# Output products of an attention and maxout kernel: one full-mode matmul, or four column tiles of 32 tokens

## The chip, the cores and the metric

The kernel runs on one core of a Trainium2 chip. The metric is device time in microseconds of one execution. A profile is taken of one execution; its span runs from the first to the last instruction of the program, and the execution's own time is a little longer.

## The reference

Two attention blocks with 32 inducing points, then a layer that takes the larger of two linear maps and multiplies it by a third.

```python
def _attn_ref(x, inducing):            # x: 4 x 12544 x 128, inducing: 32 x 128
    def mab(q, kv):
        s = scale * (q @ kv.transpose(0, 2, 1))
        a = np.exp(s - s.max(-1, keepdims=True))
        a /= a.sum(-1, keepdims=True) + 1e-09
        return a @ kv
    h = mab(I, x)                      # 32 rows a batch
    return mab(x, h)                   # 12544 rows a batch
def _moe_ref(x, w1, w2, w_out):        # x: 50176 x 128, w1, w2: 128 x 1024, w_out: 1024 x 128
    g = np.maximum(x @ w1, x @ w2)
    return g @ w_out
```

## The kernel before

max(a, b) = a + relu(b - a), so the result is x @ (w1 @ w_out) + relu(x @ (w2 - w1)) @ w_out. The kernel works with `w21 = w2 - w1` and `w1out = w1 @ w_out`. As the second attention's output is a weighted sum of the 32 rows of `h`, `h @ w21` (`hwd`) and `h @ w1out` (`m1`) are made once a batch, and the exponentials `e2` of the second attention's scores are multiplied by them without being divided first; the divisor `rp` is applied when the output leaves PSUM, since relu commutes with a positive factor.

For each of the 4 batches the first pass (`pool_scores` L356, `pool_turn` L395, `pool_accum` L414, in batch 0 `p1_transpose` L276, `p1_scores` L292, `p1_accum` L319 and L328) makes `h`, and the small steps `pool_rest` L380, `small_rep` L459, `small_h` L489, `small_hwd` L521 and `small_m1` L554 make what the second pass needs. For batches 1 to 3 this is woven into the second pass of the batch before.

The second pass goes over blocks of up to 16 chunks of 128 tokens; a block has four quarters, one for each strip of 32 rows of the TensorE array. Its steps are these.

- `stage` (L657, column tiles): scores of a block, then the exponentials on ScalarE.
- `phase` (L1085, row tiles 32 x 128): up to four relu inputs `hwd` x `e2` at once, one for each quarter; the linear part `m1` x `e2` of an output group (`linear_of`) rides along in such a phase or, for the last groups, in `linear_full` (L909). Each result is evicted from PSUM with a relu, by ScalarE (L1102) or VectorE (L1105).
- `final_one` (L932): one output product, 128 tokens of relu by one block of 128 rows of `w_out`, added to its group's PSUM bank. The relu tile is the stationary operand, so the output has tokens on partitions. A group of w chunks takes 8 w such products. There are 3,136 of them: 392 chunks by 8.
- `evict_group` (L964, or L971): the group leaves PSUM multiplied by `rp` and is stored (L989).
- `dens` (L764) makes divisors on TensorE for a few blocks; for the others `turn_e2` does it by a DMA transpose (L711) and additions on GpSimd (L720, L724).

The order on TensorE is written out by hand in `ORDER`, a list of words: `p3.2` is a phase with three jobs (and a mask that moves evictions between ScalarE and VectorE), a number is that many calls of `final_one`, `s` a stage, and the other letters are the steps named above. A `Clock` keeps estimated times of all engines while the program is recorded: its constants `PAIR` (one product) and `SWITCH` (a change of the array's tile shape) add up TensorE's time, and from the estimates the planner picks the PSUM bank, the engine of each eviction, the order of the matmuls within a phase, whether a linear part is ready, and whether `keep_busy` puts filling matmuls (L891) into a wait.

Of the kernel before, what the change touches and what calls it, by code (L numbers as in the profile page):

```python
# [20 lines left out]
class Clock:  # L21


    PAIR = 0.0558
    SWITCH = {"full": 0.11, "row": 0.097, "col": 0.097}
    LAT = 0.20
    ROW = 0.224
# [19 lines left out]
    def run(self, us, mode="full", ready=0.0, why="data"):  # L47
        if mode != self.mode:
            self.pe += self.SWITCH[mode]
            self.busy["sw"] = self.busy.get("sw", 0) + self.SWITCH[mode]  # L50
            self.mode = mode
# [80 lines left out]
def kernel(  # L132
# [9 lines left out]
    nc = tc.nc  # L142
# [3 lines left out]
    NJB = J // 128  # L146
# [22 lines left out]
    ck = Clock()  # L169
    uid = [0]  # L170

    def bank(shape, dtype=F32, only=None):
        i = min(range(8), key=lambda j: ck.bank[j]) if only is None else only
        uid[0] += 1
        return i, psum.tile(shape, dtype, name=f"ps{uid[0]}", tag=f"bank{i}", bufs=1)
# [55 lines left out]
    woutp = consts.tile([128, NJB, C], F16, name="woutp")  # L231
# [6 lines left out]
    with tc.manual_schedule(engines={ET.PE, ET.DVE, ET.Activation, ET.Pool, ET.SP}):  # L238
# [402 lines left out]
        state = {}  # L641
# [107 lines left out]
        def dens(blk):  # L749

            blks = [blk]
            if 0 < blk.index < len(blocks) - 1:
                nxt = blocks[blk.index + 1]
                if nxt.staged is not None and nxt.staged <= ck.pe and nxt.rp is None:
                    blks.append(nxt)
            bi, ps = bank([128, 512])
            ck.wait(ck.bank[bi], "den bank")
            uid[0] += 1
            rp = rpp.tile([128, 8, 4], F32, name=f"rp_{uid[0]}", tag="rp")
            n = 0  # L760
            for blk in blks:
                wd = blk.width
                for t in range(wd):
                    nc.tensor.matmul(  # L764
                        out=ps[:, 4 * (n + t) : 4 * (n + t) + 4],
                        lhsT=blk.e2[:, 128 * t : 128 * (t + 1)],
                        rhs=ones_q,
                        start=True,
                        stop=True,
                    )  # L770
                blk.rp = rp[:, n : n + wd, :]
                n += wd
            end = ck.run(0.029 * n)
            nc.vector.reciprocal(out=rp[:, 0:n, :].rearrange("p t q -> p (t q)"), in_=ps[:, 0 : 4 * n])
            ck.bank[bi] = ck.on_dve(end, 0.18 + 0.001 * 4 * n)
# [103 lines left out]
        def keep_busy(until):  # L879

            g = groups[state["g"]] if state["g"] < len(groups) else None
            if held:
                g = held[0]
            elif g is None or not g.started:
                return
            turn = ck.SWITCH["full"] if ck.mode != "full" else 0.0
            n = int((until - ck.pe - turn - 0.1) / 0.11)
            if n < (3 if turn else 1):
                return
            for _ in range(n):  # L890
                nc.tensor.matmul(  # L891
                    out=g.ps[:, 0 : 128 * min(2, len(g.chunks))],
                    lhsT=warm[:, 0:128],
                    rhs=warm[:, 0 : 128 * min(2, len(g.chunks))],
                    start=False,
                    stop=False,
                    skip_group_check=True,
                )
            ck.run(0.11 * n)
# [3 lines left out]
        def linear_full():  # L903

            g = held[0]
            if st[g.blk.b].get("m1r", INF) > ck.pe or "m1" not in st[g.blk.b]:
                return False
            for s, (q, t) in enumerate(g.chunks):
                nc.tensor.matmul(  # L909
                    out=g.ps[:, 128 * s : 128 * (s + 1)],  # L910
                    lhsT=g.blk.e2[:, 128 * t : 128 * (t + 1)],
                    rhs=m1bd[:, q, :],
                    start=False,
                    stop=True,
                    skip_group_check=True,
                )
            evict_group(held.pop(0), ck.run(0.056 * len(g.chunks)))
            return True

        def final_one():  # L920
            g = groups[state["g"]]
            n = len(g.chunks)
            if g.blk.rp is None:
                dens(g.blk)
            if g.ps is None:
                g.bank, g.ps = bank([128, 512])
                ck.wait(ck.bank[g.bank], "group bank")
                ck.bank[g.bank] = INF
            jb, t = g.order[state["mm"]]
            c = g.chunks.index((g.q, t))  # L930
            w4 = g.blk.quarters[g.q].w
            nc.tensor.matmul(  # L932
                out=g.ps[:, 128 * c : 128 * (c + 1)],
                lhsT=g.blk.relu[g.q][:, 128 * (jb * w4 + t) : 128 * (jb * w4 + t + 1)],
                rhs=woutp[:, jb, :],
                start=not g.started,
                stop=(state["mm"] + 1 == n * NJB and g.linear),
                skip_group_check=True,
            )
            g.started = True  # L940
            end = ck.run(ck.PAIR)
            state["mm"] += 1
            state["done"] += 1
            if state["mm"] == n * NJB:
                if g.linear:
                    evict_group(g, end)
                else:
                    held.append(g)
                    if g.full:
                        linear_full()  # L950
                state["g"] += 1
                state["mm"] = 0

        def evict_group(g, end):
            n = len(g.chunks)
            uid[0] += 1
            osb = outp.tile([128, 4, C], F32, name=f"o_{uid[0]}", tag="o")
            q, t0 = g.chunks[0]
            who = int(EVICT[g.index])
            m = (n, 0)[who]  # L960
            end = max(end, g.blk.divided, ck.stored.pop(0))
            done = 0.0
            if m:
                nc.vector.tensor_mul(  # L964
                    osb[:, 0:m, :],
                    g.ps[:, 0 : m * C].rearrange("p (s c) -> p s c", s=m),
                    g.blk.rp[:, t0 : t0 + m, q : q + 1].broadcast_to((128, m, C)),
                )
                done = ck.on_dve(end, 0.066 + m * 128 / 960.0)
            for k in range(m, n):  # L970
                nc.scalar.activation(  # L971
                    out=osb[:, k, :],
                    in_=g.ps[:, k * C : (k + 1) * C],
                    func=AF.Copy,
                    scale=g.blk.rp[:, t0 + k, q : q + 1],
                )
                done = max(done, ck.on_act(end, 0.25))
            ck.bank[g.bank] = done
            runs = []
            for s, (q, t) in enumerate(g.chunks):  # L980
                qu = g.blk.quarters[q]
                c = qu.c0 + t
                if runs and runs[-1][0] == qu.b and runs[-1][1] + runs[-1][3] == c:
                    runs[-1][3] += 1
                else:
                    runs.append([qu.b, c, s, 1])
            for b, c, s, m in runs:
                stored = ck.on_sp(ck.bank[g.bank], 0.6)
                nc.sync.dma_start(out=outr[b, :, c : c + m, :], in_=osb[:, s : s + m, :])  # L989
            ck.stored.append(stored)  # L990
# [40 lines left out]
        def phase(n, flip=0):  # L1031
# [9 lines left out]
            if ck.mode != "row":  # L1041
                if got:
                    keep_busy(got[0][5] - ck.SWITCH["row"])
                ck.pe += ck.SWITCH["row"]
                ck.mode = "row"
# [112 lines left out]
        for word in ORDER.split():  # L1158
            if word == "s":
                stage(blocks[state["stage"]])  # L1160
                state["stage"] += 1
            elif word.isdigit():
                for _ in range(int(word)):
                    ready = final_ready()
                    keep_busy(ready)
                    ck.wait(ready, "relu")
                    final_one()
            else:
                WORK[word[0]](*[int(n) for n in word[1:].split(".") if n])
# [32 lines left out]
```

## Time and profile before

| | |
|---|---|
| median of 2 runs | 318.06 us (317.67 to 318.45) |
| profiled execution | 317.76 us |
| its span | 316.0 us |
| TensorE busy | 308.6 us, 98% |
| ScalarE, VectorE, GpSimd busy | 280.2, 274.5, 125.8 us |
| granted TensorE clock, mean | 0.998 |
| products (L932) | 3,136 matmuls, 219 ns each, 203.5 us busy |
| relu evictions | 470 on ScalarE (627 ns), 314 on VectorE (684 ns) |

Busy time counts each stretch of time once, however many matmuls overlap in it. A single matmul's duration is a modelled latency; the time that it costs in a row of matmuls is the distance from one start to the next.

### The profile page before, as it was taken

What the parts mean: (1) busy time and instruction counts of PE and PEld (TensorE: products, weight loads), DVE (VectorE), ACT (ScalarE), POOL (GpSimd) and SP (SyncE); (2) the same over time, 40 slices, a digit from 0 to 9 for tenths busy, and PEclk for the clock granted to TensorE, in tenths of its full rate; (3) what the DMA queues carried; (4) which work ended last, traced back from release to release, by engine and by line L of the source; (5) the groups of instructions that cost most, each with busy time, mean ns of one, the idle gap of its engine ahead of it and who ended that gap; (6) DMA issues with size and microseconds to landing.
All of it is one profiled execution on the core that took longest, in us unless ns stands there. A gap on an engine that the chain in (4) does not pass through costs nothing.

```text
span 316.0 us, 12577 instructions
## 1 busy us (share of the span) xinstructions
PE 308.6 (98%) x5308; PEld 239.9 (76%) x5308; DVE 274.5 (87%) x488; ACT 280.2 (89%) x580; POOL 125.8 (40%) x187
## 2 busy tenths in 40 slices
PE   6998999999999999999999999999999999999996
PEld 3885777777877777778877787887868777788885
DVE  2468999999878999988999899989899889999885
ACT  3669999999999999998999989899999999998891
POOL 7363060666620066067510064674406564461500
PEclk9999999999999999999999999999999999999999
DMA  8999999989799999898499999897323233324232
GB/s 203 208 252 205 207 219 146 207 229 230 127 218 245 245 183 174 190 233 207 121 225 252 213 227 215 204 174 203 106 85 118 100 106 118 119 88 140 102 120 101
DMA packets 81336, 55.81 MB, mean 177 GB/s; under 512 B 62816, under 2 KB 66176, under 8 KB 81280
## 3 DMA queue, kind: packets, MB, share of 16 engines
q1 hardware_dynamic: 75312, 41.32, 55.8%
q0 software_dynamic: 5968, 13.70, 22.4%
q8 instruction: 41, 0.67, 0.9%
q14 instruction: 15, 0.12, 0.1%
HBM read 27.28 MB, written 25.69 MB: 168 GB/s over the span
## 4 chain that ended last, share of the span: by engine, by line
PE 94%; DMA 2%; ACT 1%; DVE 1%; issue 1%; POOL 0%; POOLq 0%
PE ps L932 60%; PE ps L1085 23%; DMA xn<-in_x_dram 2%; PE ps L657 2%; PE ps L356 2%; PE ps L414 2%; PE ps L276 1%; PE ps L328 1%; PE ps L292 1%; PE ps L521 0%; DVE relu L1105 0%; PE ps L319 0%; ACT e L669 0%; DVE o L964 0%; ACT e_first L696 0%
## 5 line engine op out<-in xcount | busy, mean ns | idle before, releaser
L1102 ACT ACTIVATE relu<-ps 128x512 f16<-128x512 f32 x470 | 241.0, 627 | 17.5 <-PE ps L1085 16.5
L1105 DVE TENSOR_SCALAR relu<-ps 128x512 f16<-128x512 f32 x314 | 199.7, 684 | 20.6 <-PE ps L1085 19.0
L932 PE MATMUL ps<-woutp,relu 128*128 128x128 f16 x3136 | 203.5, 219 | 0.2
L932 PEld LDWEIGHTS <-relu 128*128 128x128 f16 x3136 | 176.6, 98 | 34.4 <-issue 28.7
L1085 PE MATMUL ps<-e,hwd 32*128 32x512 f16 (+2 forms) x840 | 82.8, 361 | 0.1
L720 POOL TENSOR_TENSOR half<-ed 128x256 f32<-128x256 f16 (+2 forms) x23 | 14.1, 613 | 145.8 <-DMA ed<-e 145.8
L724 POOL TENSOR_TENSOR rd<-den,minus 128x16 f32<-128x16 f32 (+2 forms) x23 | 60.7, 2639 | 1.8
L964 DVE TENSOR_TENSOR o<-ps,rd 128x512 f32<-128x512 f32 (+3 forms) x83 | 53.2, 643 | 3.9 <-PE ps L1085 2.8
L1085 PE MATMUL ps<-m,e 32*128 32x128 f16 x372 | 36.8, 216 | 0.0
L1085 PEld LDWEIGHTS <-hwd 32*128 32x128 f16 x880 | 26.7, 91 | 12.8 <-issue 3.8
L1085 PEld LDWEIGHTS <-e 32*128 32x128 f16 x372 | 22.4, 92 | 10.4 <-issue 2.7
L720 POOL TENSOR_TENSOR half<-half 128x32 f32<-128x32 f32 (+3 forms) x69 | 22.3, 323 | 5.4
L195 POOL DMA_DIRECT2D xn<-in_x_dram x32 | 17.6, 563 | 5.7 <-DMA xn<-in_x_dram 4.3
L280 DVE COPY xT<-ps 128x512 f16<-128x512 f16 (+3 forms) x12 | 5.7, 485 | 8.6 <-PE ps L276 8.6
L964 DVE TENSOR_TENSOR o<-ps,rp 128x512 f32<-128x512 f32 (+3 forms) x20 | 12.8, 642 | 0.0
L369 ACT ACTIVATE eu<-ps 128x512 f16<-128x512 f32 x18 | 11.0, 617 | 0.6 <-PE ps L356 0.3
L669 ACT ACTIVATE e<-ps 128x512 f16<-128x512 f32 (+2 forms) x21 | 11.1, 607 | 0.3 <-PE ps L657 0.2
L283 ACT COPY xT<-ps 128x768 f16<-128x768 f16 (+3 forms) x10 | 5.7, 574 | 4.3 <-PE ps L276 4.2
L276 PE MATMUL ps<-identity,xn 128*128 128x128 f16 x98 | 7.6, 220 | 1.4 <-DMA xn<-in_x_dram 0.9
L657 PE MATMUL ps<-xT,hT 128*32 128x512 f16 (+3 forms) x110 | 8.1, 361 | 0.1
L276 PEld LDWEIGHTS <-xn 128*128 128x128 f16 x98 | 5.5, 97 | 2.9 <-DMA xn<-in_x_dram 1.2
L356 PE MATMUL ps<-xT,inducingT 128*32 128x512 f16 x72 | 6.8, 386 | 0.0
(110 smaller groups left out, 117.7 us busy)
## 6 DMA issues: line engine op xcount, KB each, us to landing
out_dram<-o SPq DMA_DIRECT2D x90, 256.0 KB, 3.0
xn<-in_x_dram POOLq DMA_DIRECT2D x24, 448.0 KB, 10.4
out_dram<-o SPq DMA_DIRECT2D x10, 128.0 KB, 2.9
wf<-in_moe_w_dram POOLq DMA_DIRECT2D x4, 256.0 KB, 6.0
xn<-in_x_dram POOLq DMA_DIRECT2D x4, 224.0 KB, 10.2
xT<-xn SPq DMA_TRANSPOSE x33, 4.4
xf<-in_x_dram SPq DMA_DIRECT2D x1, 512.0 KB, 3.7
xf<-in_x_dram SPq DMA_DIRECT2D x1, 384.0 KB, 4.2
```

The lines of the kernel that those rows point to most:

```text
L195: nc.gpsimd.dma_start(out=xn_at[b, i][:, 0:n, :], in_=xr[b, :, k0 : k0 + n, :])
L276: nc.tensor.transpose(ps[:, j, :], xn[:, g + j, :], identity16)
L356: nc.tensor.matmul(out=ps[32 * g : 32 * (g + 1), :], lhsT=inducingT, rhs=xT_tiles[b % 2][:, U * u + 4 * g : U * u + 4 * (g + 1), :], start ...
L657: nc.tensor.matmul(out=ps[32 * q : 32 * (q + 1), 128 * t : 128 * (t + n)], lhsT=hq, rhs=xT[:, c : c + n, :], start=True, stop=True, tile_p ...
L669: nc.scalar.activation(out=blk.e2[:, 0 : 128 * wd], in_=ps[:, 0 : 128 * wd], func=AF.Exp, scale=st[0]["rs"] if blk.b == 0 else scale,)
L720: nc.gpsimd.tensor_tensor(out=dst, in0=cur[:, :, 0:n], in1=cur[:, :, n : 2 * n], op=ALU.add)
L724: nc.gpsimd.tensor_tensor(out=rp[:, 0:wd, :].rearrange("p t q -> p (t q)"), in0=den[:, 0 : 4 * wd], in1=minus1[:, 0 : 4 * wd], op=ALU.pow,)
L932: nc.tensor.matmul(out=g.ps[:, 128 * c : 128 * (c + 1)], lhsT=g.blk.relu[g.q][:, 128 * (jb * w4 + t) : 128 * (jb * w4 + t + 1)], rhs=woutp ...
L964: nc.vector.tensor_mul(osb[:, 0:m, :], g.ps[:, 0 : m * C].rearrange("p (s c) -> p s c", s=m), g.blk.rp[:, t0 : t0 + m, q : q + 1].broadcas ...
L1085: nc.tensor.matmul(**seq.pop(0))
L1102: nc.scalar.activation(out=dst, in_=src, func=AF.Relu)
L1105: nc.vector.tensor_scalar(out=dst, in0=src, scalar1=0.0, scalar2=None, op0=ALU.max)
```

## The change

In `final_one` the product of 128 tokens is made by four matmuls. Each takes 32 of the 128 stationary columns (32 tokens), sits in its own strip of 32 columns of the array, and writes its own 32 partitions of the same PSUM region. All four stream the same 128 x 128 block of `w_out`. The clock's estimate of a product changes from 0.0558 to 0.0565, and its array mode from full to column, so that the planner's choices are made with these.

```diff
     PAIR = 0.0558
+    COLS = 0.0565
...
-            nc.tensor.matmul(
-                out=g.ps[:, 128 * c : 128 * (c + 1)],
-                lhsT=g.blk.relu[g.q][:, 128 * (jb * w4 + t) : 128 * (jb * w4 + t + 1)],
-                rhs=woutp[:, jb, :],
-                start=not g.started,
-                stop=(state["mm"] + 1 == n * NJB and g.linear),
-                skip_group_check=True,
-            )
+            lhsT = g.blk.relu[g.q][:, 128 * (jb * w4 + t) : 128 * (jb * w4 + t + 1)]
+            flags = {
+                "start": not g.started,
+                "stop": state["mm"] + 1 == n * NJB and g.linear,
+                "skip_group_check": True,
+            }
+            rows = [(32 * i, 32 * (i + 1)) for i in range(4)]
+            for lo, hi in rows:
+                nc.tensor.matmul(
+                    out=g.ps[lo:hi, 128 * c : 128 * (c + 1)],
+                    lhsT=lhsT[:, lo:hi],
+                    rhs=woutp[:, jb, :],
+                    tile_position=(0, lo),
+                    **flags,
+                )
             g.started = True
-            end = ck.run(ck.PAIR)
+            end = ck.run(ck.COLS, "col")
```

## The prediction

> **What bounds the kernel now.** I read the head of the page first, then the chain that ended last, then the groups by form, then the timeline.
>
> ```profile
> span 316.0 us, 12577 instructions
> PE 308.6 (98%) x5308; PEld 239.9 (76%) x5308; DVE 274.5 (87%) x488; ACT 280.2 (89%) x580; POOL 125.8 (40%) x187
> ...
> DMA  8999999989799999898499999897323233324232
> ...
> q8 instruction: 41, 0.67, 0.9%
> ...
> PE 94%; DMA 2%; ACT 1%; DVE 1%; issue 1%; POOL 0%; POOLq 0%
> ```
>
> TensorE holds 94% of the chain that ended last, and the biggest part of it (60% of the span, by the page's chain by line) is line 932, the output products that are changed here. So whatever a product costs more comes out at the end, 3,136 times. DMA is at nine tenths for the first 60% of the span and at a quarter after it. Queue q8 brings instructions: 41 packets, 0.67 MB.
>
> The groups by form (count, then busy us and mean ns of one) hold an operation of exactly the new shape: L414, 128 rows by 32 columns, 128 elements wide.
>
> ```profile
> L932 PE MATMUL ps<-woutp,relu 128*128 128x128 f16 x3136 | 203.5, 219 | 0.2
> ...
> L414 PE MATMUL ps<-xn,eT 128*32 128x128 f16 x288 | 5.7, 220 | 0.0
> ...
> L932 PEld LDWEIGHTS <-relu 128*128 128x128 f16 x3136 | 176.6, 98 | 34.4 <-issue 28.7 <-DVE relu L1105 0.3
> ...
> L414 PEld LDWEIGHTS <-eT 128*32 128x32 f16 x288 | 4.3, 96 | 1.1 <-DMA eT<-eu 0.2
> ```
>
> The 219 ns are a latency; matmuls overlap, so the price is the step from start to start, which the timeline gives (start, length, engine, line, count):
>
> ```profile
> 74.92 0.20 PE L380 MATMUL ps<-inducingT,xT 128*128 128x32 f16 x2
> ...
> 75.05 0.46 PEld L414 LDWEIGHTS <-eT 128*32 128x32 f16 x32
> 75.06 0.63 PE L414 MATMUL ps<-xn,eT 128*32 128x128 f16 x32
> ...
> 75.62 0.76 PE L1085 MATMUL ps<-e,hwd 32*128 32x512 f16 x7
> ...
> 149.93 1.85 PE L932 MATMUL ps<-woutp,relu 128*128 128x128 f16 x30
> 151.71 0.39 PE L1085 MATMUL ps<-e,hwd 32*128 32x512 f16 x4
> ```
>
> L932: (1.85 - 0.22) / 29 = 56 ns a product. L414: (0.63 - 0.22) = 0.41 us from the first to the last start; the four tiles of a quad start within 0.01 us, so 7 steps in 0.40 us: 57 ns a quad. Four column tiles run side by side and cost what one full matmul costs. The single records agree closer than two digits can: away from switches a full product steps 55.82 ns, a quad 55.83 ns, in all nine bursts of L414; after a switch the first step is 66 ns in both.
>
> **The change part by part.** *Products.* 3,136 matmuls and weight loads go, 12,544 of each come. By the single records 3,136 x (55.83 - 55.82) = 0.0 us; by the rounded timeline 3,136 x 1 ns = 3 us. I take 0 and keep 3 for the range.
>
> *Weight loads.* Three more per product lie beside the running quad, as L414's do: its 32 loads span 0.46 us while its 32 matmuls run. Without that cover a load would be serial: the nearest row is L292, 14 pairs of load and 32-wide matmul in 0.51 us, (0.51 - 0.18) / 13 = 25 ns a pair, so four pairs would be 100 ns a product. I take L414, which has the shape. [...]
>
> *Mode switches.* TensorE pauses where the tile shape changes. L932's 30th product starts at 149.93 + 1.85 - 0.22 = 151.56, L1085 at 151.71: 0.15 us in place of 0.056, and the first step after a switch is 10 ns longer: 0.10 us a switch. The same pause stands between full and column mode (the second L380 starts at 74.95, L414 at 75.05) and, by the single records, between column and row mode (0.15 us from L414's last start to L1085). The built order has 339 changes of shape now and 353 after: the 266 between products and L1085 stay, only with another shape; 29 between products and the column matmuls of L356, L414, L657 vanish; 43 come, since the small full-mode steps (L380, L459, L489, L521, L554, L764, L909) now stand between column products. +14 x 0.10 = +1.4 us.
>
> *Planner.* The clock that places the work now counts 56.5 ns a product and the column switch. In the built order no wait is added, and the stages, stores and transposes keep their order on TensorE and in SP's and POOL's queues; two filling matmuls (L891) drop out; some parallel row matmuls change places; 8 relu evictions go from ScalarE (470 to 462) to VectorE (314 to 322). By L1105's 684 ns that is 5.5 us more for an engine with 13% idle. If each delayed TensorE by its whole length it would be +5.5 us, and each could as well spare as much; most evictions hide behind the products that follow, so I take +0.5.
>
> *Instructions.* TensorE's stream grows from 10,605 to 29,417 instructions. 41 packets for 10,605 are about 256 each, so 115 packets will be fetched, 74 more. 0.9% of 16 engines' 316 us are 45.5 us, 1.1 us a packet: 81 us more for the DMA engines, 1.6% of them. It collides with the x loads while DMA is full; the tightest column-matmul waits (L414 for eT) have 0.2 to 1 us in hand. A lost microsecond at each of three batches would be +3; I take 0, since most transposes land over 1.5 us early. That packets arrive late is a rival.
>
> *Sum:* 0 + 1.4 + 0.5 = +1.9 us on the profiled execution's 317.76 (span 316.0 and 1.8 around it): 319.7. The median of the runs is 0.3 higher, so 320.0.
>
> **The rivals.** *Instruction supply (slower).* 29,417 instructions in 318 us are one packet per 2.75 us, in dense runs of products one per 256 / 8 x 56 ns = 1.8 us; now it is one per 7.7 us. If TensorE holds only the packet that it runs and the next, each must be asked for and land within the use of one. A packet's own 1.1 us fits; the round trip is not shown. The nearest rows are the stores, 3.0 us from issue to landing, and the transposes ed<-e, 3.5 us. For: the packet records show the starts scatter by several us against TensorE's progress while DMA is full. Against: the longest TensorE has ever waited on "issue" is under 1 us, and the tiles of a burst start 3 ns apart. Price: (3.0 - 2.75) x 115 = 29 us, 348 us; with 3.5 us 86 us, 405; decisive from 2.75 us a packet. [...]
>
> *Issue or load rate.* L414 shows its 6.4 ns an instruction over 64 only; they may have stood in a queue. The longest stretches without that doubt are L292 and L328, 12.5 ns. If that is the limit, 29,417 x 12.5 = 368 us, up to 3,136 x (100 - 56) more, 456, if nothing is run ahead. Against: the last quad of a burst is no later than the first.
>
> *Stalls from the moved evictions and the busier DMA.* All upper bounds together: 1.4 + 3 + 5.5 + 3 = 13, 331 us; half of it, 325, is past the 2%.
>
> *Faster.* Only if the 266 switches between products and L1085 were shorter in column mode. A fifth of each, 266 x 0.02 = 5 us, gives 315, still within 2%; the records show 146 ns from a narrow row matmul to either shape.
>
> *It does not do what it says:* the built order has 12,544 matmuls at that line, so no.
>
> **How the numbers follow.** Forecast 0.53; instruction supply 0.29; issue or load rate 0.09; added stalls over 2% 0.07; faster by 2% 0.02. About 2% is what a measurement of this kernel can tell from no change. Faster 0.02, same 0.53, slower 0.45. The forecast's own range is 317 to 324: 0 to 3 + 3 of the bounds above 318. For 8 in 10 the range must reach into instruction supply: up to 365 it leaves out the issue rate and the worst third of supply, some 18%; below 316.5 some 2%.
>
> **What would show each step.** Right: the product line with x12544, steps of 56 ns a quad from run to run, a span within 3 us of 316, q8 at about 115 packets, PE still over 90% of the chain. Supply: gaps inside runs of products, put down to "issue" or to nothing, at every 256th TensorE instruction, more of them in the first 200 us where DMA is full. Issue rate: an even step of about 100 ns after the first quads of each run, in the last third as well. Evictions: waits on L1102 and L1105 before row matmuls. The forecast is wrong if products step over 58 ns on average, or if switches differ by more than 0.02 us.

## The result and the profile after

| | before | after |
|---|---|---|
| median | 318.06 us | 480.03 us (477.03 to 483.03, 2 runs) |
| ratio | | 1.509, 95% interval 1.468 to 1.551 |
| profiled execution, its span | 317.76, 316.0 us | 483.03, 480.4 us |
| granted TensorE clock, mean | 0.998 | 0.948 |

The change makes the kernel half as slow again; 480.03 lies far outside the predicted 316.5 to 365. From here on the lines of `final_one`, `phase` and the ScalarE eviction are L941, L1093 and L1110, moved by the lines that the diff adds (in half and late one line further; in clock_only one line behind those of the kernel before).

The page of the kernel after, in its own order: span, busy time, the span in 40 slices (clock and DMA), the instruction queue, the chain by engine, and the two groups of the products (busy us, mean ns of one, idle time before them with what ended it).

```profile
span 480.4 us, 31389 instructions
PE 349.3 (73%) x14714; PEld 258.2 (54%) x14714; DVE 285.3 (59%) x496; ACT 282.8 (59%) x572; POOL 125.8 (26%) x187
...
PEclk9988998899779999999979889889999999999999
DMA  8995899345916799323956497384222123223222
...
q8 instruction: 114, 1.87, 1.7%
...
PE 67%; issue 26%; DMA 2%; ACT 2%; DVE 1%; POOL 1%; POOLq 0%; ACTq 0%
...
L941 PE MATMUL ps<-woutp,relu 128*32 128x128 f16 x12544 | 239.4, 228 | 108.0 <-issue 106.2
...
L941 PEld LDWEIGHTS <-relu 128*32 128x32 f16 x12544 | 194.1, 101 | 159.5 <-issue 153.4
```

No other engine has become the bound: each is busy for about as long as before, so its share has fallen. "Issue" has gone from 1% to 26% of the chain, and 106 us of TensorE's idle time stand ahead of products and are ended by "issue": everything that the profile knows of had been there, and the engine did not start. Queue q8 brought 114 packets; 115 were foretold.

The chain of waits summed up for TensorE says how that time is cut (us in total, times, longest us):

```profile
PE ps L941 <- issue: 106.2, 88, 3.7
PE ps L1093 <- issue: 8.8, 6, 3.3
PE ps L415 <- issue: 4.8, 5, 1.4
PE ps L941 <- ACT relu L1110: 1.5, 1, 1.5
PE ps L1093 <- DVE o L972: 1.5, 2, 0.9
...
PE ps L1093 <- ACT relu L1110: 0.7, 1, 0.7
```

The idle time ahead of products is 88 pieces of a little over a microsecond, and no even slowing. Waits on evictions come to 3.7 us in four pieces. The timeline of TensorE in the last tenth of the kernel after, where DMA is at two tenths and the granted clock is 1.00 (start, length, engine, line, count, and idle time before it):

```profile
460.68 0.96 PE L941 MATMUL ps<-woutp,relu 128*32 128x128 f16 x53
462.93 0.63 PE L941 MATMUL ps<-woutp,relu 128*32 128x128 f16 x31 [1.29 <-issue]
463.49 0.40 PE L1093 MATMUL ps<-e,hwd 32*128 32x512 f16 x7
463.81 1.36 PE L941 MATMUL ps<-woutp,relu 128*32 128x128 f16 x84
...
466.72 1.91 PE L941 MATMUL ps<-woutp,relu 128*32 128x128 f16 x122
469.87 0.23 PE L941 MATMUL ps<-woutp,relu 128*32 128x128 f16 x2 [1.24 <-issue]
```

Inside a burst 122 matmuls, 30.5 products, take 1.91 us: (1.91 - 0.22) / 30.25 = 56 ns a product, as predicted. Then everything stands still in the middle of a run of products. The count of instructions, a weight load and a matmul for each unit, tells where. In the single records I numbered TensorE's instructions. The stops lie at numbers that are 184 to 193 over a multiple of 256. Around these places the kernel after has 106 gaps of more than 0.25 us from one start to the next, 148 us together; at the same spacing shifted by half a page, as a control, it has 7 with 2.2 us. The kernel before has 5 with 1.5 us, and 3 with 0.9 us in the control. So 145 of the 164 us that the span grew stand at the ends of pages of 256 instructions.

From one page's end to the next the records show 4.02 us on average over the 111 pages after 25 us, 446 us of the 480; the median is 3.745 us. In the kernel before a page lasted 7.4 to 7.5 us on average, some 5.2 at the least. The q8 packets between two stops divide the period: median 1.16 us from TensorE's resuming to the start of the next packet, 1.09 us for the packet, 1.39 us from its end until TensorE goes on. The three medians add up to 3.64 us. In each of the 100 periods between two stops there is one packet; it starts 0.7 us or more after TensorE has resumed, and TensorE goes on 1.2 to 2.1 us after it has landed. I read this order so: a packet starts only after TensorE has stepped into a new page, and TensorE does not get past that page's end before the packet has landed.

### The profile page after: what moved, and what is told of

The parts are those of the page before. It is cut to its first block, busy times and chain, and to the rows that moved or that the text cites. A ratio compares the mean times of both kernels' runs of the same rounds, so it can differ in the third digit from the quotient of the medians.

```text
span 480.4 us, 31389 instructions
## 1 busy us (share of the span) xinstructions
PE 349.3 (73%) x14714; PEld 258.2 (54%) x14714; DVE 285.3 (59%) x496; ACT 282.8 (59%) x572; POOL 125.8 (26%) x187
## 4 chain that ended last, share of the span: by engine, by line
PE 67%; issue 26%; DMA 2%; ACT 2%; DVE 1%; POOL 1%; POOLq 0%; ACTq 0%
PE ps L941 45%; PE ps L1093 16%; DMA xn<-in_x_dram 2%; ACT relu L1110 1%; PE ps L658 1%; PE ps L415 1%; DVE relu L1113 1%; PE ps L357 1%; POOL xn L196 1%; DVE o L972 0%; PE ps L522 0%; PE ps L277 0%; PE ps L460 0%; PE ps L329 0%; ACT e L670 0%
## 5 line engine op out<-in xcount | busy, mean ns | idle before, releaser
L1110 ACT ACTIVATE relu<-ps 128x512 f16<-128x512 f32 x462 | 241.5, 604 | 159.6 <-PE ps L1093 158.1
L941 PE MATMUL ps<-woutp,relu 128*32 128x128 f16 x12544 | 239.4, 228 | 108.0 <-issue 106.2
L941 PEld LDWEIGHTS <-relu 128*32 128x32 f16 x12544 | 194.1, 101 | 159.5 <-issue 153.4
L1113 DVE TENSOR_SCALAR relu<-ps 128x512 f16<-128x512 f32 x322 | 205.5, 684 | 114.3 <-PE ps L1093 113.5
L1093 PE MATMUL ps<-e,hwd 32*128 32x512 f16 (+2 forms) x840 | 85.8, 376 | 3.5 <-DVE o L972 1.5
L1093 PE MATMUL ps<-m,e 32*128 32x128 f16 x372 | 38.9, 221 | 7.5 <-issue 7.5
L1093 PEld LDWEIGHTS <-hwd 32*128 32x128 f16 x880 | 27.1, 93 | 18.0 <-issue 10.5
L1093 PEld LDWEIGHTS <-e 32*128 32x128 f16 x372 | 23.5, 94 | 21.8 <-issue 14.0
L415 PE MATMUL ps<-xn,eT 128*32 128x128 f16 x288 | 6.8, 220 | 4.8 <-issue 4.8
L415 PEld LDWEIGHTS <-eT 128*32 128x32 f16 x288 | 4.9, 96 | 4.6 <-issue 4.2
```

The costliest lines, as they stand in the source:

```text
L415: nc.tensor.matmul(out=ps[32 * g : 32 * (g + 1), 0:128], lhsT=eT[:, 4 * (v % 2) + j, 32 * g : 32 * (g + 1)], rhs=xn_of(b, U * v + 4 * g + ...
L941: nc.tensor.matmul(out=g.ps[lo:hi, 128 * c : 128 * (c + 1)], lhsT=lhsT[:, lo:hi], rhs=woutp[:, jb, :], tile_position=(0, lo), **flags,)
L1093: nc.tensor.matmul(**seq.pop(0))
L1110: nc.scalar.activation(out=dst, in_=src, func=AF.Relu)
L1113: nc.vector.tensor_scalar(out=dst, in0=src, scalar1=0.0, scalar2=None, op0=ALU.max)
```

## The experiments

The theory was: instructions come in pages of 256 (114 packets for 29,417 instructions), the packet that lets the next page start is on its way while one runs (it starts 1.16 us after TensorE's resuming), and a page cannot be had faster than this loop, 3.64 us by its three medians (supply). The rivals were a TensorE limit for each instruction (issue rate), weight loads that are slower than the bursts show, and a cost of each column product or mode change. In the table, "lost at page ends" is the sum of the gaps over 0.25 us at these places less that of the control half a page off.

| kernel | TensorE instructions | q8 packets | median us | lost at page ends, us |
|---|---|---|---|---|
| before | 10,605 | 41 | 318.0 | 0.6 |
| late_third | 12,669 | 49 | 322.1 | 4.7 |
| mixed | 13,287 | 52 | 321.9 | 4.6 |
| cols64 | 16,873 | 66 | 340.3 | 10.4 |
| late | 17,709 | 69 | 372.4 | 54.4 |
| half | 19,917 | 77 | 362.5 | 27.0 |
| after | 29,417 | 114 | 480.0 | 146 |

The order of late and half is the point to see: more instructions and less time. It is the density of instructions that counts, not their number.

### Two tiles of 64 columns

```diff
-            rows = [(32 * i, 32 * (i + 1)) for i in range(4)]
+            rows = [(64 * i, 64 * (i + 1)) for i in range(2)]
```

> Each product is two column tiles of 64 tokens in place of four of 32: column mode everywhere, but 16,873 TensorE instructions instead of 29,417. Instruction supply (a page of 256 instructions takes 3.5 to 4.0 us to come, one page ahead at most): 66 pages in 318 us are 4.8 us a page, 64 products a page last 3.6 us in a dense run; so nearly hidden, 320 to 335 us, short waits at some page ends in the first 200 us. Issue rate of 12.5 ns an instruction: 4 in 56 ns are 14 ns, so 318 to 322. [...]

Measured: 340.25 us (338.35 to 341.45), ratio 1.069 (1.066 to 1.073). From the page, the chain and the products:

```profile
PE 82%; DMA 8%; DVE 4%; issue 3%; ACT 1%; SPq 0%; POOL 0%; POOLq 0%; DVEq 0%
...
L941 PE MATMUL ps<-woutp,relu 128*64 128x128 f16 x6272 | 209.0, 220 | 7.7 <-issue 7.5
```

Two loads and two matmuls for a product still fit into its 56 ns: idle time before products is 7.7 us in all, and weight loads that cost more, product by product, are out. It ended 5 us above the range of supply. A page now holds 64 products, 64 x 55.8 = 3.57 us in a dense run, about the length of the loop, and it is lost or not with DMA: set against the kernel before product by product, 16.2 of the 19.8 us had been lost by 190 us, where DMA is full. Page ends account for some 10 us and the planner for some 3 (below). Of the rest, 2 us lie in the first step of a run of products: 80 ns where it was 66, in 149 runs. Another 1.6 us are TensorE's waits for transposes (1.1 for `eT`, 0.5 for `xT`). Some 3 us are not settled.

### Quads in every second group, and quads in the last groups only

```diff
+            quad = g.index % 2 == 1        # half
+            quad = g.index >= 66           # late: the last 1,184 products
+            rows = [(32 * i, 32 * (i + 1)) for i in range(4)] if quad else [(0, 128)]
...
+            end = ck.run(ck.COLS, "col") if quad else ck.run(ck.PAIR)
```

> Every second output group (1,552 of 3,136 products... by the built order 1,552 with four tiles, 1,584 full) is made by four column tiles, the others by full matmuls; 19,917 TensorE instructions. A cost per product (slow loads, or 100 ns a product by the issue rate) gives half of the 162 us: 390 to 400. Instruction supply is not linear: 78 pages in 318 us are 4.1 us each, just above the 3.5 to 4.0 us of a page, so 330 to 355, with waits only at page ends.

> Only the last 1,184 products (output groups 66 and later, from about 211 us on, where DMA is 0.43 busy) are four column tiles. If packets come late only because the DMA engines are full, there is nothing to wait for here: 318 to 325. If the fetch loop itself is 3.5 to 3.75 us a page, the 10,635 instructions from there on are 41.5 pages, 145 to 156 us where 101 are needed now: 360 to 375, with a gap at every 256th instruction. A cost per product of 44 to 51 ns also gives 370 to 378, but evenly, without gaps.

Measured: half 362.48 us (362.06 to 362.90), ratio 1.140 (1.138 to 1.142); late 372.40 us (371.99 to 372.82), ratio 1.171 (1.169 to 1.173). Late lies in the range of supply; half ended 7 us above it. The chain of half:

```profile
PE 81%; issue 6%; DMA 5%; ACT 3%; DVE 2%; SPq 1%; POOL 0%; POOLq 0%; DVEq 0%; ACTq 0%
```

With quads in every second group dense stretches alternate with thin ones, and half of the products cost 44 us and not the 81 that half of 162 would be. That the loop catches up in the thin stretches fits this, but is not shown by itself. Of the 44 us, 27 stand at page ends. Another 8 are no supply at all: 79 times a run of products changes between a quad and a full matmul, and each of these steps takes 0.15 us in place of 0.056. The other 9 us are not settled. Of late, the page shows the slices, the instruction queue and the products:

```profile
PE   8989999999999999999999966787676776767674
...
DMA  8999999998998999499999863122222131221212
...
q8 instruction: 69, 1.13, 1.3%
...
L942 PE MATMUL ps<-woutp,relu 128*32 128x128 f16 (+1 forms) x6688 | 212.4, 220 | 40.4 <-issue 40.2
```

TensorE is full up to slice 23 and at six to eight tenths from where the quads begin, with DMA at one to three tenths. By product, late runs within 0.2 us of the kernel before up to product 1,900; from there it falls behind evenly, to 54 us at the end, and all of that stands at page ends. The 42 pages after 200 us last 3.82 us on average. So the loop needs no contention to be too slow; a DMA that is full (the rival of a merely crowded fetch) is not the cause.

### Synthetic products behind the kernel

Behind the whole kernel, 512 quads on a constant tile, then 2,048 full-mode matmuls 32 wide, then 2,048 that are 96 wide; nothing reads the results.

```diff
+        for _ in range(512):
+            for i in range(4):
+                nc.tensor.matmul(out=ps[32 * i : 32 * (i + 1), 0:128], lhsT=warm[:, 32 * i : 32 * (i + 1)],
+                                 rhs=warm[:, 0:128], start=True, stop=True, tile_position=(0, 32 * i), ...)
+        for _ in range(2048):
+            nc.tensor.matmul(out=ps[:, 0:32], lhsT=warm[:, 0:128], rhs=warm[:, 0:32], start=True, stop=True)
+        for _ in range(2048):
+            nc.tensor.matmul(out=ps[:, 0:96], lhsT=warm[:, 0:128], rhs=warm[:, 0:96], start=True, stop=True)
```

> The kernel before, with three stretches of TensorE work behind its end whose results nobody reads, 16 pages of 256 instructions each: 512 quads of column tiles (56 ns a quad), 2,048 pairs of weight load and 32-wide full matmul (25 ns a pair), 2,048 pairs with a 96-wide one (43 ns a pair). No other engine or data DMA works then. Instruction supply: the first two both come at the fetch loop's pace, 3.5 to 3.75 us a page (1.8 and 3.2 us of work), 56 to 60 us each, in bursts with a gap at each page; the third at its own 5.4 us a page, 87 us, without gaps. Issue rate 12.5 ns: first and second 51 us each, evenly. [...]

Measured: 520.3 us (one run); from the single records the three parts took 57.1, 60.0 and 87.0 us. First the groups by form (the added matmuls), then the timeline of the quads:

```profile
L1187 PE MATMUL ps<-warm 128*128 128x96 f16 x2048 | 87.2, 206 | 0.0
...
L1185 PE MATMUL ps<-warm 128*128 128x32 f16 x2048 | 54.0, 177 | 6.1 <-issue 5.6
...
L1175 PE MATMUL ps<-warm 128*32 128x128 f16 x2048 | 32.9, 224 | 24.5 <-issue 24.5
```

```profile
313.01 2.46 PE L1175 MATMUL ps<-warm 128*32 128x128 f16 x161
317.14 1.97 PE L1175 MATMUL ps<-warm 128*32 128x128 f16 x128 [1.67 <-issue]
320.60 1.97 PE L1175 MATMUL ps<-warm 128*32 128x128 f16 x128 [1.48 <-issue]
324.32 1.97 PE L1175 MATMUL ps<-warm 128*32 128x128 f16 x128 [1.76 <-issue]
```

Each burst is 128 loads and 128 matmuls, one page, and takes 1.97 us; the next ones start 3.46 and 3.72 us after the one before. Nothing waits on data here, no mode changes and DMA is at 3%. The 32-wide matmuls are in full mode, with no column tile: alone they would need 25 ns a pair, and they get 60.0 us for 16 pages, 3.75 us a page. The 96-wide ones use 5.44 us a page and stop nowhere. The limit belongs to the page, not to column tiles. Issue rate and slow loads fall: a limit for each instruction would have given even steps, and within a burst the 256 instructions start 7 ns apart on average.

The same quads with 24 more DMA transposes on SP's queue beside them (the two other loops left out):

```diff
+        for n in range(24):
+            i = n % 7
+            nc.sync.dma_start_transpose(
+                xT_tiles[n // 7 % 2][:, P1 * i : P1 * (i + 1), :], xn_at[B - 1, i][:, 0:P1, :]
+            )
...
```

> The kernel before, then 512 quads of column tiles (16 pages) whose results nobody reads, while 24 DMA transposes of the size of an x transpose run on SP's queue. If a full DMA delays the instruction packets, pages that come while transposes run take over 4 us, up to 6 as in the first 200 us of the changed kernel, and those after them 3.5 to 3.75; if not, all take 3.5 to 3.75 us, 57 us in all as without the transposes.

Measured: 383.18 us (one run), the quads took 67.3 us. Two windows, of the kernel without and with the transposes (us, busy time by engine with counts, clock, DMA share, GB/s):

```profile
314.00:370.00 56.00, 31.53 (x1982) 29.27 (x1974) 0.00 (x0) 0.00 (x0) 0.00 (x0) 0.97 0.03 8
```

```profile
314.00:381.00 67.00, 37.07 (x1976) 34.38 (x1964) 0.00 (x0) 0.00 (x0) 0.00 (x0) 0.85 1.07 170
```

With DMA full a page lasts 4.55 us in the median, against 3.73. The packet itself is no longer (0.94 against 1.08 us); what grows is the time from TensorE's resuming to the packet's start, 2.14 us against 1.14. The wait is ahead of the transfer. The granted clock is lower here too, 0.85 against 0.97, but it is not the cause: between 333.3 and 343.5 us the records have it full, and the pages from 333.6 and 337.8 us last 4.28 and 5.10 us. The pages of the kernel after agree in the large: 4.12 to 4.31 us on average in each part of the first 300 us, where DMA is at 0.59 to 0.82, and 3.64 us after 400, where it is at 0.24. Within the first 300 us they do not follow the DMA share.

### The planner's clock alone, and the quads without it

```diff
-            end = ck.run(ck.PAIR)
+            end = ck.run(ck.COLS, "col")     # clock_only, with full matmuls; quads_oldclock is the reverse
```

> The planner's clock counts a product as in the changed kernel (56.5 ns, column mode), but the products are full matmuls as before: the moved evictions and order alone (8 relu from ScalarE to VectorE). By the prediction's step +0.5 us, 0 to +5.5: 318 to 319, at most 323.5.

> The whole change with the planner's clock as before (PAIR, full mode), so that evictions and phases are placed as in the kernel before. Page supply: 115 pages of about 4.0 us set the time, whatever the planner does: 477 to 481 us, the planner's 3 us vanish among the page waits. If the planner's choices add on the critical path of TensorE as they do in the clock-only kernel: 3 us below the changed kernel, 476 to 477. If the planner's choices made the stalls (evictions that come late): under 400 us.

Measured: clock_only 321.13 us (320.68 to 323.82), ratio 1.010 (1.006 to 1.015); quads_oldclock 486.13 us (485.03 to 487.02), ratio 1.528 (1.525 to 1.530). The planner's new choices cost 3.1 us by themselves. The largest loss, 1.1 us, is seen in VectorE's timeline of clock_only, where L1106 is the relu eviction:

```profile
86.32 1.89 DVE L1106 TENSOR_SCALAR relu<-ps 128x512 f16<-128x512 f32 x3 [0.38 <-PE ps L1086]
88.12 0.21 DVE L492 COPY hT<-ps 128x128 f16<-128x128 f16 x1
```

The same place in the kernel before:

```profile
85.92 0.69 DVE L1105 TENSOR_SCALAR relu<-ps 128x512 f16<-128x512 f32 x1 [0.45 <-PE ps L1085]
86.53 0.21 DVE L491 COPY hT<-ps 128x128 f16<-128x128 f16 x1
```

Three evictions stand ahead of the copy `hT`; in the kernel before it was one. `small_hwd` waits 1.0 us for the copy. Five losses of 0.4 to 0.5 us at other places make up most of the rest. With quads the old clock helps nothing; the time lies 5 us above what was expected. The chain of quads_oldclock:

```profile
PE 69%; issue 26%; ACT 2%; DMA 2%; DVE 1%; POOL 0%; POOLq 0%; DVEq 0%
```

A page lasts 4.06 us in place of 4.02, and 152 us stand at page ends. The evictions did not make the stalls.

### Quads where they save a mode change

Mixed uses quads in the 447 products that stand between two phases together with column matmuls and no full-mode step (the planner's clock as before); late_third in every third run of products from group 66 on, 344 products.

```diff
+            if set(kinds) & set("sca") and not set(kinds) & set("rehwmHW"):   # mixed
+                quads.update(range(lo + 1, hi))
...
+            return state["g"] >= 66 and nth[n] % 3 == 0                       # late_third
```

> Four column tiles only for the 447 products (of 3,136) that stand between two phases together with column matmuls (stages, pool scores, pool sums) and no full-mode step; the planner's clock is that of before, so all other instructions keep their order. 26 mode changes fewer (337 to 311 by line), 13,287 TensorE instructions, 52 pages. Instruction supply: 6 us a page on average, at 160 extra instructions a run some single pages come late; -26 x 0.10 = -2.6 us and at most +2 of waits: 315 to 318. A cost of 44 to 51 ns for each product in column tiles: +20 to 23 - 2.6, 335 to 338.

> Four column tiles in every third run of products from output group 66 on (344 products), the planner's clock as before; 335 mode changes (337 before), 12,669 TensorE instructions. Instruction supply: a run of 20 quads is 160 instructions, less than a page, and the two full runs behind it let the next page come: 317 to 320, no or few waits at page ends. A cost of 44 to 51 ns for each product in column tiles, whatever its cause: +15 to 18, 333 to 336.

Measured: mixed 321.87 us (320.80 to 323.55), ratio 1.012 (1.009 to 1.015); late_third 322.14 us (320.65 to 322.89), ratio 1.011 (1.008 to 1.015). Both miss the expectation, by 4 and by 2 us, and both for a reason of the theory: a few page ends fall late. One of mixed:

```profile
105.53 1.12 PE L941 MATMUL ps<-woutp,relu 128*32 128x128 f16 x65
107.96 0.63 PE L941 MATMUL ps<-woutp,relu 128*32 128x128 f16 x31 [1.30 <-issue]
```

Sixteen products in a row are enough here (in the kernel before, DMA is at 0.98 from 100 to 200 us): the page that ends here had 4.9 us of work in it and lasted 6.2. In late_third the time lost against the kernel before, product by product, lies in four jumps of 0.7 to 1.6 us, all of them at instructions 187 over a multiple of 256, and all else keeps pace within 0.2 us. The largest is no product's at all: it falls on two 1-wide matmuls of `pool_accum` (L434), behind a run of 27 quads and the column matmuls that follow it. So a quad has no cost of its own, or the 344 of them would have lost 15 us.

### A version without the stretches that lost time

Mixed20 leaves six stretches of mixed out, those around its losses.

```diff
+            if before_ in (795, 1221, 1399, 1412, 1713, 1876):
+                continue
```

> Quads in 20 of the 26 stretches of the mixed kernel (336 products, 12,621 TensorE instructions, about 50 packets); the six stretches left out are those behind or before which the mixed kernel lost time (at 106.6, 147, 160 to 170, 190 us). Page supply: each stretch saves one switch, 20 x 0.10 = 2.0 us, if no page end falls late: 316 to 317 us, ratio 0.994 to 0.997. If quads cost time of their own (a step over 55.8 ns, about 2.5 us per hundred products by the half and late kernels taken evenly): 326 us. If the losses of the mixed kernel were not at these places but come with any quads: 319 to 321.

Measured: 318.40 us (317.83 to 319.11), ratio 1.0005 (0.9992 to 1.0018). No difference, so nothing here beats the kernel before. There is no stop inside its runs of products any more. At the 20 stretches' edges, 11 came out 0.07 to 0.16 us earlier and 5 0.09 to 0.13 us later, 0.7 us net in place of the 2.0 hoped for, and in the profiled execution one wait gave back more:

```profile
76.32 1.24 PE L941 MATMUL ps<-woutp,relu 128*32 128x128 f16 x76
78.54 0.63 PE L415 MATMUL ps<-xn,eT 128*32 128x128 f16 x32 [0.98 <-DMA eT<-eu]
```

Mixed is the same program up to its product 795, and in its profile the products keep pace with the kernel before at this place (product 515). So this wait differs from one execution to the next, and the quads are not shown to be its cause.

## Why the prediction was wrong

The step that failed is *Instructions*, in its words: "I take 0, since most transposes land over 1.5 us early. That packets arrive late is a rival." It costed the 74 more packets as a load on the DMA engines, 1.6%, and not as a chain that TensorE itself waits in. The right picture was in the text, as the rival *Instruction supply*, with 0.29 against the forecast's 0.53; its signs ("gaps inside runs of products, put down to 'issue' ... at every 256th TensorE instruction") are what the profile after shows. Only that there would be more of them in the first 200 us did not come true: by 204 us 63 us had been lost, and 101 in the 276 us behind. Two things put it in second place and made it small.

The round trip was mis-sized. The rival took 3.0 us from the stores, hence 29 us in all, with 3.5 us as the worse case. The loop has 3.64 (kernel after, behind 400 us, DMA at 0.24) to 3.75 us (tail, DMA at 0.02 to 0.03) with DMA nearly idle, and 4.55 with DMA full (tail_dma). The store row ends when its data land; it has nothing for the 1.39 us after that until TensorE resumes. The row that ended nearest was the one called the worse case: 3.5 us gave 405. The form of the price was not at fault: with the measured page of 4.02 us, (4.02 - 2.75) x 115 = 146 us, as much as was lost at page ends. Counted in pages, 111 x 4.02 = 446 us after the first 25 make 480 in all, with the last part of a page and the store; this is an account and no test, since the 4.02 are taken from the same pages.

The evidence held against it had no force. "The longest TensorE has ever waited on issue is under 1 us" was read from a kernel whose pages last 7.4 us on average, twice the loop; little there could have shown it. The bursts of 64 instructions were a quarter of a page. The ends of pages cost next to nothing at 7.4 us a page, 1.5 us in five gaps in the kernel before; in the kernel after, where the work of a dense page is 1.8 us and the loop takes 3.64, they cost 148 us / 106 = 1.4 us each.

Point by point, the other steps:

- *Products:* 55 to 56 ns from quad to quad inside the bursts at full clock, as predicted.
- *Weight loads:* hidden. Late and the synthetic quads show no cost outside the page ends, and the 56 ns of a quad in the bursts hold its four loads and four matmuls; four pairs one after the other, at the 25 ns of L292, would be 100 ns.
- *Mode switches:* about 0.10 us, seen singly at the edges of mixed20 and in the 79 changes inside half's runs. The count of +14 is not tested alone.
- *Planner:* +0.5 was too little; 3.1 us measured, inside the bound of 5.5 that stood beside it. I took it for hidden because most evictions are (in the kernel before TensorE waits for one, 0.3 us); the two put ahead of `hT` were not.
- *Contention:* a wait of this size stands once in mixed20, 0.98 us for eT; that the instruction packets caused it is not shown. It is small beside the pages.
- *Issue rate* is refuted by the bursts: over whole pages the instructions start 7 ns apart on average, not 12.5, and then all stop.

The lower clock, 0.948, is not a matter of the number of stops: late has 46 and keeps 0.998, half has 28 and 0.986. In the kernel after the records have the clock at one half in twelve stretches, 50 us of the span together; a quad steps 107 ns there, and at least 12 of the 18 us or so that do not stand at page ends lie in them. The clock does not make the pages long: those without such a stretch still last 4.05 to 4.14 us on average in the first 300 us. In tail, with DMA nearly idle, the page from 328.33 us ran almost whole at half clock and lasted 3.73 us, as long as the others.

## What to carry to other kernels

Count TensorE's instructions before splitting a matmul: take the stretch's instructions by 256 and hold the time of such a page against some 3.7 us (3.73 in tail), or 4.5 where DMA is full (4.55 in tail_dma; single pages took up to 6.2, in mixed). Where the work of a page was far less than that, as the 1.8 us of dense quads here, TensorE stood still at nearly every page's end (106 gaps in some 115 pages, 148 us), whatever the array could do; the split into four tiles was free in array time here (56 ns a quad) and was paid in instructions. The kernel before, whose pages last 7.4 us, twice the loop, shows nothing of it, and a short burst shows it only where a page's end falls badly (mixed, late_third). So look for a stretch that is as dense as the one planned, and as long, or bound the time by pages times loop.

## What the runs showed of the hardware

- In the dense stretches of tail TensorE went through pages of 256 instructions no faster than one per 3.45 to 4.0 us with DMA nearly idle, 13.5 to 16 ns an instruction, weight loads counted. In the kernel after four single pages took 2.8 to 3.3 us, three of them right behind one of over 4 us. The periods in the quiet stretches come in steps of 0.274 us (3.47, 3.745, 4.02).
- Of the loop, 1.16 us pass before the packet starts, 1.09 us in it, and 1.39 us between its landing and TensorE's going on (medians of the kernel after). In tail_dma full DMA lengthened only the first, to 2.14 us.
- Full-mode matmuls are held by it too: in tail, pairs with 32-wide matmuls ran at 60.0 us / 2,048 = 29 ns, where their step inside a burst is 25 ns.
- A change between full and column mode inside a run of products costs 0.15 us in place of 0.056 (79 times in half).
